# Moving the four block sums of each quad from VectorE to GpSimd in the last third of a fused attention + two-MoE kernel

## The chip, the cores and the metric

The kernel runs on one core of one Trainium2 chip. The metric is the device time of one execution in microseconds (us), taken as the median of several runs. The trace is of one profiled execution; its engines are called PE (TensorE matmuls; PEld its weight loads), DVE (VectorE), ACT (ScalarE), POOL (GpSimd) and SP (SyncE, which issues the DMAs here).

## What is computed

An attention without a score matrix feeds a first MoE layer (softplus) and a second one (ELU). The change lies in the last product, `g @ w_out` of the second layer:

```
def _moe2_ref(x, w_in, w_out) -> np.ndarray:
    h = x @ w_in
    alpha = 1.0
    g = np.where(h > 0.0, h, alpha * (np.exp(np.minimum(h, 0.0)) - 1.0))
    return (g @ w_out).astype(np.float32)
```

There are 2304 tokens, `d_model` is 512 and `d_ff` is 2048; everything is float32.

## The kernel before

Tokens are cut into six blocks of 384 (`BLK`), and the blocks into three pairs; `d_ff` is cut into eight slices of 256. One pair with one slice is a *quad*. Each layer goes pair by pair and, within a pair, slice by slice. A float32 product is done as three products of rounded halves (high by high, high by low, low by high), so each operand is split by a cast on ACT (the high half) and a subtraction on DVE (the low half).

The products with `w_in` (`add_up`, matmuls at L833) use a 2x2 block scheme with seven products in place of eight. In the second layer, the second and third pair (the trace calls them by p = 1 and 2; the change's words call them pairs 2 and 3) use such a scheme for `w_out` too. For these sixteen quads `add_elu` leaves g as two tiles of two blocks each, (B11, B21) and (B12, B22), 128x384 a block. `add_parts` then makes the seven left operands: three are blocks of g as they are, and four come from sums, done in place: S = B21 + B22 and B21 <- B11 - B21 ahead of product 7, B11 <- S - B11 ahead of product 6, and B12 <- B12 - B11 ahead of product 3 (L1116, one instruction each, both inputs in SBUF). Each operand is then split into a tile of a ring of six called F: the cast at L1135 (ACT), the subtraction at L1139 (DVE). `add_products` multiplies them by the ready right operands (matmuls at L1185, nine to an operand, in threes: two that read its high half, then one that reads its low half) in the order 1, 7, 6, 2, 5, 4, 3, for four quads at a time, so that the same six F tiles come round again and again: a tile is refilled when PE has used it, and used again five operands later. The four S tiles hold S until product 5.

The tiles live in memory that other rings have finished with, and the trace names them by those: the F tiles are `claim_q`, `claim_xq`, `claim_yl`, `claim_st`, `claim_k`, `claim_v`; the g tiles are `claim_u`, `claim_g`, `claim_gh`, `claim_gl`, `claim_ti`; S is `claim_raw` or `claim_y`. `claim_raw` is also the output tile, into which L1208 (ACT) and L1210 (DVE) bring the finished products from PSUM.

The other work of a quad that shares the engines: L846 and L852 (ACT) copy products of `w_in` out of PSUM, L867 (DVE) adds such a copy to a product in PSUM, L946 and L950 (ACT) and L960 (DVE) make the ELU, L603 (ACT), L607 and L614 (DVE) prepare the next pair's input.

Each step is recorded with an engine, an estimated duration (`t_dve`, `t_pool`), what it reads, writes and holds, and a due time. `Plan.order` then lists all steps: at each turn the step that can start first on its engine, late ones ahead. That list is the order of each engine's queue; on the chip each engine works in its order and waits on semaphores.

Of the kernel before, what the change touches and what calls it, by code (L numbers as in the profile page):

```python
# [15 lines left out]
PE, ACT, DVE, POOL, DMA = "PE", "ACT", "DVE", "POOL", "DMA"  # L16
# [130 lines left out]
def t_act(n, psum=False):  # L147
    return (0.051 if psum else 0.093) + n / 1200


def t_dve(n, fast=False):
    return 0.069 + n / (1920 if fast else 960)


def t_pool(n):
    return 0.15 + n / 476
# [7 lines left out]
def attention_moe_moe_kernel(  # L164
# [30 lines left out]
    nc = tc.nc  # L195
# [5 lines left out]
    BLK = P * R  # L201
# [40 lines left out]
    def step(eng, dur, r=(), w=(), make=(), due=None, after=0.0, behind=(), port=False, hold=(), line=None, tab=None):  # L242


        def add(fn):
            n = plan.add(eng, dur, fn, r, w, make, due, after, [*behind, last.get(line)], port, hold, tab)
            if line is not None:
                last[line] = n
            return n

        return add
# [818 lines left out]
    def slot(key):  # L1070
        T[key] = views[plan.tile_ring[key], plan.place[key]]
        return T[key]
# [17 lines left out]
    def halves(key):  # L1090


        slot(key)
        one = views.get(("F1", plan.place[key]))
        T[key] = (one, T[key]) if one is not None else (T[key][:, :BLK], T[key][:, BLK:])
        return T[key]
# [4 lines left out]
    def add_parts(m, p, i, f):  # L1101


        gk = [("g", m, p, f, j) for j in range(2)]
        sk, fk = ("S", m, p, f), ("F", m, p, f, i)
        A = [("A", m, p, f, n) for n in range(4)]
        b11, b21, b12, b22 = A
        block = lambda n: T[gk[n // 2]][:, n % 2 * BLK : (n % 2 + 1) * BLK]
        if i == 1:
            for n, key in enumerate(A):  # L1110
                plan.writer[key] = plan.writer[gk[n // 2]]

        def sum_(out, x, y, op, r, w, hold, make=()):
            @step(DVE, t_dve(BLK), r=r, w=w, make=make, hold=hold)
            def _():
                nc.vector.tensor_tensor(out(), x(), y(), op=op)  # L1116

        s = lambda: T[sk]
        if i == 7:
            sum_(lambda: slot(sk), lambda: block(1), lambda: block(3), ALU.add, [b21, b22], [], gk, [(sk, "S")])  # L1120
            sum_(lambda: block(1), lambda: block(0), lambda: block(1), ALU.subtract, [b11], [b21], gk[:1])
        if i == 6:
            sum_(lambda: block(0), s, lambda: block(0), ALU.subtract, [sk], [b11], gk[:1])
        if i == 3:
            sum_(lambda: block(2), lambda: block(2), lambda: block(0), ALU.subtract, [b11], [b12], gk)
        key, get, hold = {
            1: (b11, lambda: block(0), gk[:1]), 7: (b21, lambda: block(1), gk[:1]), 6: (b11, lambda: block(0), gk[:1]),
            2: (b12, lambda: block(2), gk[1:]), 5: (sk, s, []), 4: (b22, lambda: block(3), gk[1:]),
            3: (b12, lambda: block(2), gk[1:]),
        }[i]  # L1130
        fh, fl = ((x, m, p, f, i) for x in ("fh", "fl"))

        @step(ACT, t_act(BLK), r=[key], make=[(fk, "F")], w=[fh], hold=hold, line="F")
        def _():
            nc.scalar.copy(halves(fk)[0], get())  # L1135

        @step(DVE, t_dve(BLK), r=[key, fh], w=[fl], hold=[fk, *hold])
        def _():
            nc.vector.tensor_tensor(T[fk][1], get(), T[fk][0].bitcast(F32), op=ALU.subtract)  # L1139
# [326 lines left out]
```

## Time and profile before

| what | value |
|---|---|
| median of 3 runs | 832.95 us (832.44 to 833.37) |
| the profiled execution: its time | 833.62 us |
| its span, first to last instruction | 831.9 us |
| mean granted TensorE clock | 0.998 of full speed |
| busy: PE, PEld | 809.3 us (97%), 732.4 us (88%) |
| busy: DVE, ACT, POOL | 657.5 us (79%), 564.7 us (68%), 6.1 us (1%) |

Shares are of the span. What lies around the span is 833.62 - 831.9 = 1.7 us. Busy times of an engine count each instruction in full, although the next one starts a little before it ends (a 128x384 instruction of DVE lasts 0.55 us, and the next one starts 0.47 us after it).

### The profile page before, as it was taken

The numbers are of one execution on the slowest core, as the hardware profiler recorded it, in microseconds if no ns is written. First come the engines' busy times: TensorE is split into PE (matmuls) and PEld (weight loads), VectorE is DVE, ScalarE is ACT, GpSimd is POOL, SyncE is SP. The second block draws the span as 40 slices with busy tenths as digits, with TensorE's granted clock in tenths as the row PEclk, the third lists the DMA queues.
The fourth block names the chain that finished last, engine by engine and source line by source line (L and its number), as shares of the span: only waits on it lengthen the run. The fifth ranks groups of instructions, "written<-read, shape, count | busy, mean of one in ns | idle before, by whom it ended". The sixth has DMA issues, their size and how long they took to land.

```text
span 831.9 us, 13270 instructions
## 1 busy us (share of the span) xinstructions
PE 809.3 (97%) x5110; PEld 732.4 (88%) x5110; DVE 657.5 (79%) x1088; ACT 564.7 (68%) x889; POOL 6.1 (1%) x28
## 2 busy tenths in 40 slices
PE   5799999999999999999999999999999999999997
PEld 4455788888889999999999998898999999999997
DVE  7879999979887768777679788968468697766775
ACT  4878987876787856756657767667466675557552
POOL 2000000000000000000000000000000000000000
PEclk9999999999999999999999999999999999999999
DMA  9597786636985556576855898987687676787563
GB/s 288 155 284 234 225 283 197 196 115 206 284 263 215 181 206 236 206 253 221 321 191 218 289 371 331 328 325 242 239 311 292 234 284 222 271 278 301 202 225 147
DMA packets 75166, 205.33 MB, mean 247 GB/s; under 512 B 18784, under 2 KB 34144, under 8 KB 65632
## 3 DMA queue, kind: packets, MB, share of 16 engines
q1 hardware_dynamic: 75104, 204.49, 71.0%
q8 instruction: 40, 0.66, 0.3%
q14 instruction: 22, 0.18, 0.1%
HBM read 143.65 MB, written 60.82 MB: 246 GB/s over the span
## 4 chain that ended last, share of the span: by engine, by line
PE 82%; DVE 8%; ACT 5%; DMA 2%; issue 2%; DVEq 0%; ACTq 0%; SPq 0%
PE ub L833 21%; PE acc L1007 15%; PE acc L1045 13%; PE uc L833 11%; PE Pb L1185 8%; PE ua L833 5%; PE Pc L1185 4%; PE Pa L1185 2%; PE px L522 1%; DMA wf_i<-wfd 1%; DVE mt L346 1%; PE acc L1040 1%; PE pk L390 1%; DMA raw_i<-in_moe_w_in_dram 1%; PE pq L506 1%
## 5 line engine op out<-in xcount | busy, mean ns | idle before, releaser
L833 PE MATMUL ub<-xf,wf_i 128*128 128x384 f32 x1104 | 226.5, 339 | 1.4 <-ACT s L846 1.1
L833 PEld LDWEIGHTS ub<-xf,wf_i 128*128 128x128 f32 x1104 | 189.3, 188 | 13.4 <-ACT s L846 4.3
L846 ACT COPY s<-ub 128x384 f32<-128x384 f32 x138 | 65.8, 477 | 72.7 <-PE ub L833 71.6
L833 PE MATMUL uc<-xf,wf_i 128*128 128x384 f32 x552 | 111.8, 337 | 0.7 <-ACT g L916 0.7
L1007 PE MATMUL acc<-gh,wo_o 128*128 128x512 f32 (+1 forms) x512 | 111.7, 340 | 0.0
L1045 PE MATMUL acc<-wo_o,gh 128*128 128x512 f32 x336 | 106.7, 398 | 0.0
L833 PEld LDWEIGHTS uc<-xf,wf_i 128*128 128x128 f32 x552 | 95.1, 188 | 5.7 <-ACT g L916 1.9
L867 DVE TENSOR_TENSOR h<-uc,s 128x384 f32<-128x384 f32 x92 | 51.1, 555 | 52.6 <-PE uc L833 47.5
L1007 PEld LDWEIGHTS acc<-gh,wo_o 128*128 128x128 f32 x512 | 82.9, 188 | 7.3
L1045 PEld LDWEIGHTS acc<-wo_o,gh 128*128 128x128 f32 x336 | 61.4, 188 | 9.0 <-ACT yt L1295 0.2
L1045 PE MATMUL acc<-wo_o,gl 128*128 128x512 f32 x168 | 66.5, 396 | 0.0
L1007 PE MATMUL acc<-gl,wo_o 128*128 128x512 f32 (+1 forms) x256 | 65.5, 336 | 0.0
L973 DVE TENSOR_TENSOR gl<-g,gh 128x768 fp32r<-128x768 f32 x60 | 57.2, 953 | 8.4 <-ACT gh L969 8.3
L833 PE MATMUL ua<-xf,wf_i 128*128 128x384 f32 x276 | 56.0, 337 | 0.0
L969 ACT CAST gh<-g 128x768 fp32r<-128x768 f32 x60 | 50.2, 836 | 7.1 <-DVE g L960 6.3
L833 PEld LDWEIGHTS ua<-xf,wf_i 128*128 128x128 f32 x276 | 47.9, 188 | 1.4 <-ACT sx L535 0.3
L746 DVE TENSOR_TENSOR wf_i<-st_i,wf_i 128x1024 fp32r<-128x1024 f32 x30 | 36.7, 1222 | 15.1 <-ACT wf_i L742 15.1
L1007 PEld LDWEIGHTS acc<-gl,wo_o 128*128 128x128 f32 x256 | 39.1, 188 | 5.3
L916 ACT ACTIVATE g<-h 128x384 f32<-128x384 f32 (+1 forms) x44 | 30.2, 686 | 16.3 <-DVE h L867 16.1
L1045 PEld LDWEIGHTS acc<-wo_o,gl 128*128 128x128 f32 x168 | 31.5, 187 | 6.8
L742 ACT CAST wf_i<-r_i 128x512 fp32r<-128x512 f32 (+1 forms) x48 | 23.2, 511 | 16.5 <-PE uc L833 16.4
L742 ACT CAST wf_i<-st_i 128x1024 fp32r<-128x1024 f32 x30 | 31.4, 1048 | 1.1 <-DVE st_i L726 1.0
(282 smaller groups left out, 1429.2 us busy)
## 6 DMA issues: line engine op xcount, KB each, us to landing
wf_i<-wfd SPq DMA_DIRECT2D x16, 1792.0 KB, 8.2
ws<-wos SPq DMA_DIRECT2D x28, 1024.0 KB, 5.4
raw_i<-in_moe_w_in_dram SPq DMA_DIRECT2D x16, 1024.0 KB, 6.5
raw_o<-in_moe_w_out_dram SPq DMA_DIRECT2D x16, 1024.0 KB, 7.4
wo_o<-wod SPq DMA_DIRECT2D x14, 1024.0 KB, 5.5
wfd<-wf_i SPq DMA_DIRECT2D x8, 1792.0 KB, 7.8
r_i<-w32i SPq DMA_DIRECT2D x24, 512.0 KB, 6.0
wod<-wo_o SPq DMA_DIRECT2D x8, 1024.0 KB, 5.2
```

The costliest lines, as they stand in the source:

```text
L346: top = lambda o, x, y: nc.vector.tensor_tensor(o, x, y, op=ALU.max)
L742: nc.scalar.copy(view(0, lo, n, c), get())
L746: nc.vector.tensor_tensor(view(1, lo, n, c), get(), view(0, lo, n, c).bitcast(F32), op=ALU.subtract)
L833: nc.tensor.matmul(ps[:, :BLK], T[wk][:, lo : lo + P], T[xk][:, (2 * c + kc) * BLK : (2 * c + kc + 1) * BLK], start=(i in first and kc == ...
L846: nc.scalar.copy(new(sk), T[key][:, :BLK])
L867: nc.vector.tensor_tensor(T[hk][:, half * BLK : (half + 1) * BLK], T[key][:, :BLK], T[sk], op=ALU.add)
L916: nc.scalar.activation(o, i, AF.Softplus)
L969: nc.scalar.copy(new(hk), T[gk])
L973: nc.vector.tensor_tensor(new(lk), T[gk], T[hk].bitcast(F32), op=ALU.subtract)
L1007: nc.tensor.matmul(ps, T[wk][:, lo : lo + P], T[g][:, cols], start=(first and n == 0 and starts), stop=(f == NQ - 1 and j == 1 and n == 2) ...
L1045: nc.tensor.matmul(ps, T[g][:, col : col + P], T[wk][:, (2 * a + j) * DM : (2 * a + j + 1) * DM], start=(first and n == 0), stop=(f == NQ ...
L1185: nc.tensor.matmul(ps[:, x * 256 : x * 256 + 256], T[fk][a][:, r * P : (r + 1) * P], T[ck][:, q * 512 + b * 256 : q * 512 + b * 256 + 256] ...
```

## The change

```
@@ -1111,9 +1111,9 @@
                 plan.writer[key] = plan.writer[gk[n // 2]]
 
         def sum_(out, x, y, op, r, w, hold, make=()):
-            @step(DVE, t_dve(BLK), r=r, w=w, make=make, hold=hold)
+            @step(POOL, t_pool(BLK), r=r, w=w, make=make, hold=hold)
             def _():
-                nc.vector.tensor_tensor(out(), x(), y(), op=op)
+                nc.gpsimd.tensor_tensor(out(), x(), y(), op=op)
 
         s = lambda: T[sk]
         if i == 7:
```

The 64 sums go to POOL, with the planner's estimate for that engine, 0.15 + 384/476 = 0.96 us in place of 0.069 + 384/960 = 0.47 us. The planner makes its list anew. Apart from the numbers in names, the queues of PE and of SP come out as before; those of DVE and ACT change places here and there.

On DVE, where the first group of four quads of the second pair turns to its product 7 (rows of the difference; - is before, a space is both):

```order
 L1139 TENSOR_TENSOR claim_v_5818<-claim_u_5885,claim_v_5818 128x384
-L1116 TENSOR_TENSOR claim_y_6255<-claim_g_5925,claim_gl_5924 128x384
 L1139 TENSOR_TENSOR claim_q_3026<-claim_g_5906,claim_q_3026 128x384
-L1116 TENSOR_TENSOR claim_g_5925<-claim_g_5925 128x384
-L1116 TENSOR_TENSOR claim_g_5906<-claim_y_6244,claim_g_5906 128x384
-L1116 TENSOR_TENSOR claim_g_5925<-claim_y_6255,claim_g_5925 128x384
 L1139 TENSOR_TENSOR claim_xq_3365<-claim_g_5925,claim_xq_3355 128x384
```

Four sums leave DVE's queue between the low halves of product 7's operands. 

On DVE, where the last quad of all reaches `w_out` (the end of the program; `claim_gh_5959` and `claim_ti_5670` are its g):

```order
 L960 SCALAR_TENSOR_TENSOR claim_gh_5959<-claim_gh_5959,h_2_7_0_7996 128x768
+L960 SCALAR_TENSOR_TENSOR claim_ti_5670<-claim_ti_5670,h_2_7_1_8063 128x768
 L1139 TENSOR_TENSOR claim_st_5666<-claim_gh_5959,claim_st_5666 128x384
-L960 SCALAR_TENSOR_TENSOR claim_ti_5670<-claim_ti_5670,h_2_7_1_8063 128x768
 L1139 TENSOR_TENSOR claim_k_5810<-claim_gl_5960,claim_k_5810 128x384
 L1139 TENSOR_TENSOR claim_v_5818<-claim_u_5885,claim_v_5818 128x384
-L1116 TENSOR_TENSOR claim_y_6255<-claim_gh_5959,claim_ti_5670 128x384
 L1139 TENSOR_TENSOR claim_q_3026<-claim_ti_5729,claim_q_3026 128x384
-L1116 TENSOR_TENSOR claim_gh_5959<-claim_gh_5959 128x384
 L1210 TENSOR_TENSOR claim_raw_5748<-Pb_2_4_0_8107,claim_raw_5748 128x2x256
 L1210 TENSOR_TENSOR claim_raw_5748<-Pb_2_4_1_8115,claim_raw_5748 128x256
 L1139 TENSOR_TENSOR claim_xq_3365<-claim_gh_5959,claim_xq_3355 128x384
```

The second half of the last quad's ELU now stands ahead of the low half for `claim_st`, and the sums between the low halves are gone.

On ACT at the same place:

```order
 L1208 COPY claim_raw_5748<-Pb_2_0_0_7495 128x2x256
+L950 ACTIVATE claim_ti_5670<-claim_ti_5670 128x768
 L1135 CAST claim_st_5666<-claim_gh_5959 128x384
-L950 ACTIVATE claim_ti_5670<-claim_ti_5670 128x768
+L1208 COPY claim_raw_5748<-Pb_2_0_1_7505 128x256
 L1135 CAST claim_k_5810<-claim_gl_5960 128x384
-L1208 COPY claim_raw_5748<-Pb_2_0_1_7505 128x256
 L1135 CAST claim_v_5818<-claim_u_5885 128x384
 L1135 CAST claim_q_3026<-claim_ti_5729 128x384
```

The exponential of the last quad's second half goes ahead of the cast for `claim_st`.

## Rows read from the trace of the kernel before

**Rows 1.** The page: busy time of each engine, share of the span, instructions.

```profile
PE 809.3 (97%) x5110; PEld 732.4 (88%) x5110; DVE 657.5 (79%) x1088; ACT 564.7 (68%) x889; POOL 6.1 (1%) x28
```

**Rows 2.** Busy time of each engine from 594 to 830 us.

```profile
core 0: us, PE busy (x) PEld busy (x) DVE busy (x) ACT busy (x) POOL busy (x), PEclk, DMA share, GB/s
594.00:830.00 236.00, 232.15 (x1644) 230.41 (x1642) 170.22 (x305) 139.79 (x256) 0.00 (x0) 1.00 0.70 255
```

**Rows 3.** All waits of PE from 590 to 832 us: total, times, longest.

```profile
PE ub L833 <- ACT s L846: 0.8, 2, 0.6
PE ub L833 <- DMA wf_i<-wfd: 0.2, 1, 0.2
```

**Rows 4.** The chain that ended last, from 795 us: start, length, what.

```profile
795.95 5.36 PE Pb L1185 x45
...
822.83 3.95 PE Pb L1185 x33
...
826.80 0.69 DVE claim_raw L1210
```

**Rows 5.** DVE's busy time, 594 to 830 us: L1116, L1139, L960, L607, L614.

```profile
594.00:830.00 236.00, 34.74 (x64) 1.00 0.70 255
...
594.00:830.00 236.00, 60.27 (x111) 1.00 0.70 255
...
594.00:830.00 236.00, 29.57 (x31) 1.00 0.70 255
...
594.00:830.00 236.00, 6.68 (x7) 1.00 0.70 255
...
594.00:830.00 236.00, 3.80 (x4) 1.00 0.70 255
```

**Rows 6.** POOL's only two-input instructions (by line); then instructions around one of them.

```profile
L461 POOL TENSOR_TENSOR q<-q,qm 128x384 f32<-128x384 f32 x4 | 3.3, 828 | 17.9 <-DVE qm L454 17.0 <-DVE qd L476 0.9
...
16.83 0.83 POOL L461 TENSOR_TENSOR q<-q,qm 128x384 f32<-128x384 f32 x1 [0.92 <-DVE qd L476]
...
17.54 0.56 DVE L491 TENSOR_TENSOR q<-q,qd 128x384 f32<-128x384 f32 x1
...
17.69 0.52 ACT L467 ACTIVATE q<-q 128x384 f32<-128x384 f32 x1 [1.22 <-POOL q L461]
```

**Rows 7.** Instructions in order of time: mid stretch, DVE and then PE.

```profile
702.38 0.56 DVE L1139 TENSOR_TENSOR claim_yl<-claim_raw,claim_yl 128x384 fp32r<-128x384 f32 x1 [0.96 <-ACT claim_yl L1135]
...
713.36 1.23 PE L1185 MATMUL Pb<-ws,claim_yl 128*128 128x256 f32 x9
```

**Rows 8.** The same, first group of the second pair: DVE, then PE.

```profile
625.36 0.55 DVE L1139 TENSOR_TENSOR claim_st<-claim_g,claim_st 128x384 fp32r<-128x384 f32 x1
...
627.71 0.55 DVE L1116 TENSOR_TENSOR claim_g<-claim_g 128x384 f32<-128x384 f32 x1
...
634.11 1.24 PE L1185 MATMUL Pc<-ws,claim_xq 128*128 128x256 f32 x9
```

**Rows 9.** The same, last quad of all: DVE, ACT, PE.

```profile
798.34 0.56 DVE L1139 TENSOR_TENSOR claim_st<-claim_gh,claim_st 128x384 fp32r<-128x384 f32 x1 [0.93 <-ACT claim_st L1135]
799.09 0.96 DVE L960 SCALAR_TENSOR_TENSOR claim_ti<-claim_ti,h 128x768 f32<-128x768 f32 x1 [0.18 <-ACT claim_ti L950]
799.96 0.55 DVE L1139 TENSOR_TENSOR claim_k<-claim_gl,claim_k 128x384 fp32r<-128x384 f32 x1
...
803.24 0.55 DVE L1139 TENSOR_TENSOR claim_xq<-claim_gh,claim_xq 128x384 fp32r<-128x384 f32 x1
...
797.33 0.57 ACT L1208 COPY claim_raw<-Pb 128x512 f32<-128x512 f32 x1
797.79 0.51 ACT L1135 CAST claim_st<-claim_gh 128x384 fp32r<-128x384 f32 x1
798.21 0.84 ACT L950 ACTIVATE claim_ti<-claim_ti 128x768 f32<-128x768 f32 x1
...
800.07 1.24 PE L1185 MATMUL Pb<-ws,claim_st 128*128 128x256 f32 x9
801.15 1.24 PE L1185 MATMUL Pc<-ws,claim_k 128*128 128x256 f32 x9
802.23 1.24 PE L1185 MATMUL Pc<-ws,claim_v 128*128 128x256 f32 x9
...
804.36 1.24 PE L1185 MATMUL Pc<-ws,claim_xq 128*128 128x256 f32 x9
```

More of the change, by code (lines that the diff above doesn't have):

```diff
@@ L1113, in sum_ @@
         def sum_(out, x, y, op, r, w, hold, make=()):
-            @step(DVE, t_dve(BLK), r=r, w=w, make=make, hold=hold)
+            @step(POOL, t_pool(BLK), r=r, w=w, make=make, hold=hold)
             def _():
-                nc.vector.tensor_tensor(out(), x(), y(), op=op)
+                nc.gpsimd.tensor_tensor(out(), x(), y(), op=op)
         s = lambda: T[sk]
```

## The prediction

> **What bounds the kernel now.** I read the busy times first: PE is busy for 97% of the span and POOL for 1% [rows 1]. Then the stretch in which the sums lie, 594 to 830 us: PE is busy for 232.15 of 236 us at full clock, DVE for 170.22, ACT for 139.79, and POOL runs nothing at all [rows 2]. A busy PE alone proves little, so I read its waits: from 590 us on PE waits three times, 1.0 us in all, for a copy on ACT and for a transfer, and never for an F tile or a sum [rows 3]. The chain that ended last says the same: from 795.95 us it is PE's w_out products back to back up to the last one at 826.8 us, then one addition and the stores [rows 4]. So the end is set by PE's own work, which the change doesn't touch. Time can only be won out of that 1.0 us, and lost where a sum on POOL, or what stands behind it, makes PE wait.
>
> **What the change removes.** 64 sums leave DVE, 34.74 us of its busy time [rows 5], or 64 x 0.47 = 30 us of its queue. None of it lies on the chain, so it is worth nothing by itself; PE's own work hides it. Were DVE the bound, those 30 us would be the gain.
>
> **What it adds.** 64 instructions on POOL. The nearest row is POOL's own subtraction of two SBUF operands of 128x384, 0.828 us (one operand is repeated along its rows, which is the difference) [rows 6]; I take 0.83 us. That is 53 us in 236 on an engine with no other work there, so its queue is never full; no DMA is issued from it. Handing over is cheap: ACT started 0.03 us after that subtraction ended (16.83 + 0.83 = 17.66, then 17.69) [rows 6]. I count 0.08 us from a DVE or POOL result to POOL.
>
> **How much delay the F tiles bear.** In the steady stretch a low half is done long before its use: one started at 702.38 us and lasted 0.56, and PE reached the tile at 713.36, 10.4 us later [rows 7]. The six F tiles are refilled as PE frees them, and a sum in the middle of a group has its operands earlier still. A sum that takes 0.83 in place of 0.55 us, or even twice that, vanishes there. Two kinds of place remain: where the last quad of a group of four has just made its g and its sums are wanted at once.
>
> *The first group.* Both operands of the last quad's S were ready at about 625.4 us, but DVE, which works in order, came to the second sum only at 627.71; PE used the tile that hangs on it, `claim_xq`, at 634.11 [rows 8]. On POOL the sum has its own queue. Suppose the worst, that POOL starts only when DVE has done the four low halves in front, at 625.36 + 4 x 0.47 = 627.3 us plus 0.08: two sums (1.74), cast (0.54) and low half (0.57) end at 630.2, 3.9 us ahead of PE. The first tile of the stretch, `claim_st` at 625.36, hangs on no sum. Cost: nothing.
>
> *The last group.* Here nothing is interleaved any more and slack is smallest: the low half of `claim_xq` ended at 803.24 + 0.55 = 803.79, and PE came to it at 804.36 [rows 9]. PE's third matmul of the nine is the first to read the low half; nine take 1.08 us (801.15 to 802.23), so 0.24 us can be added to each slack. With the new order: ACT runs the exponential at 797.33 + 0.46 = 797.79, DVE the ELU at about 798.67, which ends at 799.62, 0.4 us earlier than before (0.96 us after 799.09). The low half of `claim_st` follows it, 799.54 to 800.09, where it ended at 798.90 before; PE needs it at 800.07 + 0.24 = 800.31. It fits by 0.2 us. Now the sums, in three cases:
> - No collision with DVE: S from 799.70 to 800.53, the second sum to 801.44, cast to 801.98, and the low half, behind two additions of L1210 that start once PE has closed `Pb` at 801.31, ends at 802.9. That is 0.9 us earlier than before.
> - POOL is kept out until DVE's four low halves end at 801.50: S and the second sum take 2 x 0.83 + 0.08, cast and low half 1.11, the end is at 804.35, and PE needs it at 804.36 + 0.24 = 804.60. Still no wait.
> - POOL gets in first and holds DVE for each whole sum: S from 800.09 to 800.92, the low half of `claim_k` ends at 801.47 where PE needs it at 801.39 (0.08 us late); a second sum then pushes `claim_v` to 802.85 against 802.55, 0.3 us late. The tiles behind have room. Cost: 0.4 us.
>
> The third and fourth sums are wanted later (product 6 and product 3 come 8 and 24 operands after product 1 in a group of four quads), and DVE has fewer instructions than before. From 0 to 0.4 us, nearer to nothing, because two of the three cases cost nothing; I take 0.1.
>
> **A rule that speaks against the change.** The only overlap of POOL with a two-input DVE instruction is 17.54 to 17.66 us, and DVE's took 0.56 us, no longer than usual [rows 6]; that is the tail of POOL's instruction and tells little. The Trainium skill, "SBUF — State Buffer", section "Who interferes with whom", states that a DVE instruction with two SBUF inputs and a GpSimd instruction that reads SBUF exclude each other for the whole instruction, whoever comes first. If it holds, the second and third case above are the true ones, and no trace shown here decides it. By rows alone it matters how much DVE work could collide: 60.27 + 29.57 + 6.68 + 3.80 = 100.3 us of two-input instructions stay on DVE [rows 5], 43% of the stretch. Even if every sum held DVE for its full 0.83 us, DVE would be taken for 170.22 - 34.74 + 53 = 188 of 236 us, or 80%: it would still keep up.
>
> **The sum.** 833.62 us for the profiled execution, minus 0 for DVE's relief, plus 0 in the steady stretch, plus 0 at the first group, plus 0.1 at the last: 833.7. The median of the runs shown lies 0.7 us below the profiled one, so 832.95 + 0.1, rounded: 833.1 us.
>
> **Rivals.**
> - *Slower: POOL's sums are much longer than its row.* The place is `claim_xq` of the last quad, the case in which POOL starts at 801.50. Two sums of T each end PE's slack when 801.50 + 2T + 1.19 passes 804.60, so at T = 0.955 us, and each us beyond costs 2 us. To pass 0.2% (1.7 us, about what a measurement of this kernel can tell from no change) T must be 1.8 us. A sum that always waited out one 768-wide ELU instruction would take 0.83 + 0.95 = 1.78: a loss of 1.65, 834.6 us. With T at three times its row, 2.5 us, the loss is 3.1, 836.1. For it: 43% of the stretch can collide. Against it: at that very place DVE has no two-input instruction to run, as it waits for the sum, and 0.83 us was steady over four instances (3.3 us in all).
> - *Faster: PE's 1.0 us of waits goes* [rows 3]. If DVE's relief brought ACT's copies forward, 832.0 us at best. Against it: two of the three waits are for L846, whose inputs come from PE, and the third for a transfer; none has a sum in front. It is also below the 0.2%.
> - *Held up in the queue of ACT.* A cast that waits for POOL stands ahead of L846 and L852, on which PE's next w_in products wait. If each of the four group ends lost 0.3 us so (a sum's excess of 0.28 over DVE's), 1.2 us: 834.2 us, still within 0.2%. For it: before, the casts behind the second sum ran right after it. Against it: POOL starts that sum earlier than DVE did.
>
> **How the numbers follow.** No change within 0.2%: 0.80 (the forecast with 0.68, the ACT queue with 0.08, part of the 1.0 us won with 0.04). Slower by more: 0.16 (T of 1.8 us or more with 0.12, several small waits on top of each other with 0.04). Faster by more: 0.04, for something that the trace doesn't show. The range reaches from 832.2 (the lowest run, 832.44, less a quarter of PE's waits) to 834.8 (the slower rival at T = 1.78 us, with 0.2 us of spread); I leave out 836 with the rest.
>
> **What would show it.** In the changed kernel's profile DVE is busy for some 35 us less, POOL for some 53 us more, and the end is the same: PE's waits from 590 us on stay near 1 us and none names L1116 or a claimed tile. The sums on POOL should last 0.83 us; if they last longer, or L1139 and L960 last longer or start late behind no semaphore, the two engines collide. In the last group the low half of `claim_xq` should end between 802.9 and 804.4 us. The prediction is wrong if PE shows waits at L1185 for ACT or DVE at 800 to 806 us, or if L846 starts late behind a cast that waits for POOL.

## The result, and the profile after

The changed kernel takes 838.42 us (median of 4 runs, 837.88 to 840.26) where the kernel before takes 833.16 (4 runs, 832.44 to 833.55): the ratio is 1.0068, with a 95% interval of 1.0050 to 1.0086. It is slower by 5 to 6 us, three times what 0.2% is, and lies above the range of 832.2 to 834.8. The profiled execution took 838.94 us with a span of 837.2, against 833.62 and 831.9 before, so the two traces show the same 5.3 us, at the same granted clock of 0.998.

The page, and the busy times of the stretch with the sums (the stretch is 5 us longer than in [rows 2] because the kernel is):

```profile
PE 811.3 (97%) x5110; PEld 732.1 (87%) x5110; DVE 647.9 (77%) x1024; ACT 564.3 (67%) x889; POOL 79.2 (9%) x92
...
594.00:835.00 241.00, 234.68 (x1646) 231.12 (x1644) 160.79 (x241) 139.88 (x257) 73.16 (x64) 1.00 0.69 249
```

64 sums have left DVE, which is 64 x 0.47 = 30 us of its queue (the records of neighbours overlap by 0.08 us, so that their 34.74 us count a little twice), yet DVE is busy for only 9.4 us less than in [rows 2] (170.22 minus 160.79). POOL is busy for 73.16 us, not 53. Where the rest of DVE's relief went shows line by line. Busy time of L1139, L960, L607, L614, and of L867, which has one operand in PSUM:

```profile
594.00:835.00 241.00, 79.16 (x111) 1.00 0.69 249
...
594.00:835.00 241.00, 30.53 (x31) 1.00 0.69 249
...
594.00:835.00 241.00, 7.57 (x7) 1.00 0.69 249
...
594.00:835.00 241.00, 4.49 (x4) 1.00 0.69 249
...
594.00:835.00 241.00, 24.87 (x45) 1.00 0.69 249
```

Against [rows 5], the same 111 low halves cost 18.89 us more, and the three other lines 0.96, 0.89 and 0.69: together 21.4 of the 30 us come back as longer instructions on DVE, which leaves 8.6, about the 9.4 seen. L867, the one with a single operand in SBUF, is no longer than it was in the kernel before:

```profile
594.00:830.00 236.00, 25.00 (x45) 1.00 0.70 255
```

**Where PE falls behind.** PE has the same instructions in the same order in both kernels, so the start of each can be taken from the start of the same one before. Before 600 us, where nothing was changed, this lag lies between -1.1 and 2.0 us in the executions of this document, so only its growth counts. It is counted from the first matmul that starts after 612 us: there the execution of the kernel before loses 0.43 us to a transfer of `wf_i` (the wait for DMA in [rows 3]), which no other execution does there, and all but 0.07 us of that is left out so. From there on it grows at three places and nowhere else: by 1.97 us from 612 to 640 (first group of the second pair), by 2.50 from 676 to 700 (the second group, where the third pair's input is prepared on DVE between the low halves), and by 0.89 from 798 to 808 (the last group). In the steady stretches between them it grows by nothing. The sum, 5.33 us with rounding, is the whole loss of the profiled execution.

PE's waits from 590 to 840 us name the first two places, and L1185 waits for nobody in this view:

```profile
PE ub L833 <- ACT s L846: 1.9, 3, 1.1
PE uc L833 <- DVE h L867: 1.0, 1, 1.0
PE ua L833 <- DVE h L867: 0.6, 1, 0.6
```

Against [rows 3] these are 3.5 us instead of 1.0, all before products of `w_in`, which hang on no sum. What they wait for is a copy or an addition that empties a PSUM bank. The view shows less than the lag because a wait inside a series of matmuls is recorded as a longer series.

**First group.** POOL, DVE, ACT and PE in order of time:

```profile
622.52 1.61 POOL L1116 TENSOR_TENSOR claim_y<-claim_g,claim_gh 128x384 f32<-128x384 f32 x1 [11.24 <-DMA out_dram<-y]
624.21 1.02 POOL L1116 TENSOR_TENSOR claim_g<-claim_g 128x384 f32<-128x384 f32 x1
625.31 1.61 POOL L1116 TENSOR_TENSOR claim_g<-claim_y,claim_g 128x384 f32<-128x384 f32 x1
626.88 1.33 POOL L1116 TENSOR_TENSOR claim_y<-claim_g,claim_gl 128x384 f32<-128x384 f32 x1
628.28 1.20 POOL L1116 TENSOR_TENSOR claim_g<-claim_g 128x384 f32<-128x384 f32 x1
...
625.97 1.37 DVE L1139 TENSOR_TENSOR claim_st<-claim_g,claim_st 128x384 fp32r<-128x384 f32 x1
627.26 1.36 DVE L1139 TENSOR_TENSOR claim_k<-claim_ti,claim_k 128x384 fp32r<-128x384 f32 x1
...
631.12 0.55 DVE L1139 TENSOR_TENSOR claim_xq<-claim_g,claim_xq 128x384 fp32r<-128x384 f32 x1
...
635.66 0.54 DVE L867 TENSOR_TENSOR h<-uc,s 128x384 f32<-128x384 f32 x1
...
629.52 0.52 ACT L1135 CAST claim_xq<-claim_g 128x384 fp32r<-128x384 f32 x1 [1.96 <-POOL claim_g L1116]
...
636.24 0.85 ACT L946 ACTIVATE claim_gl<-h 128x768 f32<-128x768 f32 x1 [1.80 <-DVE h L867]
...
638.54 0.49 ACT L846 COPY s<-ub 128x384 f32<-128x384 f32 x1
...
626.88 1.61 PE L1185 MATMUL Pb<-ws,claim_st 128*128 128x256 f32 x9
...
634.65 1.24 PE L1185 MATMUL Pc<-ws,claim_xq 128*128 128x256 f32 x9
639.09 1.15 PE L833 MATMUL ub<-xf,wf_i 128*128 128x384 f32 x5 [1.11 <-ACT s L846]
```

The same L867 and the same series of PE in the kernel before:

```profile
633.66 0.55 DVE L867 TENSOR_TENSOR h<-uc,s 128x384 f32<-128x384 f32 x1
...
626.70 1.24 PE L1185 MATMUL Pb<-ws,claim_st 128*128 128x256 f32 x9
```

While POOL runs sums back to back, each low half on DVE lasts 1.37 us instead of 0.55, one starting every 1.3 us, and each sum 1.2 to 1.6 us instead of the 1.02 us that a sum lasts alone. The extra 0.82 us has no releaser: it lies inside DVE's instruction. The first of these low halves is that of `claim_st`, which PE wanted at once: its series of nine takes 1.61 us instead of 1.24, so 0.37 us of the 1.97 are lost at a tile that hangs on no sum. Then the casts: ACT stands 1.96 us for the last quad's second sum. The low half of that operand ended at 631.67, and PE reached the tile at 634.65, so the tile itself was 3 us early, as predicted. But two L867 stood behind that low half in DVE's queue. The second started at 635.66 (633.66 before), the activation L946 behind it waited 1.80 us, and behind that in ACT's queue stood the copy L846 for which PE then waited; the lag grows by 1.38 us there. The remaining 0.28 us come at 620 us, where an L867 starts 0.43 us after the product that it waits for (0.08 before). The lag grows as much there in e3 below, in which nothing collides; the cause is open. (0.37, 1.38 and 0.28 are 2.03; the 0.07 of the transfer goes off.)

**Last group.** DVE, POOL, PE:

```profile
803.09 0.96 DVE L960 SCALAR_TENSOR_TENSOR claim_ti<-claim_ti,h 128x768 f32<-128x768 f32 x1 [1.26 <-ACT claim_ti L950]
803.96 0.55 DVE L1139 TENSOR_TENSOR claim_st<-claim_gh,claim_st 128x384 fp32r<-128x384 f32 x1
804.43 1.37 DVE L1139 TENSOR_TENSOR claim_k<-claim_gl,claim_k 128x384 fp32r<-128x384 f32 x1
805.73 1.36 DVE L1139 TENSOR_TENSOR claim_v<-claim_u,claim_v 128x384 fp32r<-128x384 f32 x1
807.01 1.36 DVE L1139 TENSOR_TENSOR claim_q<-claim_ti,claim_q 128x384 fp32r<-128x384 f32 x1
...
804.13 1.26 POOL L1116 TENSOR_TENSOR claim_y<-claim_gh,claim_ti 128x384 f32<-128x384 f32 x1 [6.85 <-DVE claim_ti L960]
805.47 1.20 POOL L1116 TENSOR_TENSOR claim_gh<-claim_gh 128x384 f32<-128x384 f32 x1
806.75 1.21 POOL L1116 TENSOR_TENSOR claim_gh<-claim_y,claim_gh 128x384 f32<-128x384 f32 x1
...
805.57 1.40 PE L1185 MATMUL Pc<-ws,claim_k 128*128 128x256 f32 x9
806.80 1.44 PE L1185 MATMUL Pc<-ws,claim_v 128*128 128x256 f32 x9
808.08 1.44 PE L1185 MATMUL Pc<-ws,claim_q 128*128 128x256 f32 x9
809.35 1.57 PE L1185 MATMUL Pc<-ws,claim_xq 128*128 128x256 f32 x9
```

Three sums and three low halves take turns. The four series of nine matmuls last 1.40, 1.44, 1.44 and 1.57 us, where three of them have 1.24 in [rows 9] and that of `claim_q` had 1.22:

```profile
803.31 1.22 PE L1185 MATMUL Pc<-ws,claim_q 128*128 128x256 f32 x9
```

PE loses 0.16 + 0.20 + 0.22 + 0.33 = 0.91 us inside the series, which is the 0.89 by which the lag grows.

### The profile page after: what moved, and what is told of

Same layout as the page of the kernel before. It is cut to its first block, busy times and chain, and to the rows that moved or that the text cites. A ratio compares the mean times of both kernels' runs of the same rounds, so it can differ in the third digit from the quotient of the medians.

```text
span 837.2 us, 13340 instructions
## 1 busy us (share of the span) xinstructions
PE 811.3 (97%) x5110; PEld 732.1 (87%) x5110; DVE 647.9 (77%) x1024; ACT 564.3 (67%) x889; POOL 79.2 (9%) x92
## 4 chain that ended last, share of the span: by engine, by line
PE 81%; DVE 11%; ACT 4%; issue 2%; DMA 1%; DVEq 0%; SPq 0%; ACTq 0%
PE ub L833 20%; PE acc L1007 14%; PE acc L1045 13%; PE uc L833 10%; PE Pb L1185 7%; PE ua L833 5%; PE Pc L1185 3%; PE Pa L1185 2%; PE acc L1040 2%; PE px L522 1%; DVE mt L346 1%; DVE xf L607 1%; DVE ts L614 1%; DMA w32i<-ti_i 1%; PE pq L506 1%
## 5 line engine op out<-in xcount | busy, mean ns | idle before, releaser
L846 ACT COPY s<-ub 128x384 f32<-128x384 f32 x138 | 65.8, 477 | 69.5 <-PE ub L833 68.3
L867 DVE TENSOR_TENSOR h<-uc,s 128x384 f32<-128x384 f32 x92 | 51.0, 554 | 56.4 <-PE uc L833 44.8
L1116 POOL TENSOR_TENSOR claim_raw<-claim_ti,claim_ti 128x384 f32<-128x384 f32 x1 | 1.0, 1021 | 376.8 <-DVE claim_ti L960 376.8
```

What stands on the lines that cost most here:

```text
L846: nc.scalar.copy(new(sk), T[key][:, :BLK])
L867: nc.vector.tensor_tensor(T[hk][:, half * BLK : (half + 1) * BLK], T[key][:, :BLK], T[sk], op=ALU.add)
```

## The experiments

The theory after this result has two parts. *Collision*: a sum on POOL and a DVE instruction with two SBUF operands exclude each other, and the low halves that are held come late or hold up what stands behind them. *Lateness*: a sum on POOL ends later than one on DVE would, and the cast or low half that waits for it holds up the copies and additions behind it on ACT and DVE, which empty PE's PSUM banks. The rival is *order*: the planner made a new list, and the list alone costs the time. A plainer rival is that POOL's work as such slows the others. Each kernel was compared with the kernel before on the same chip (833.25 us for e1 to e4, 832.56 for e5 to e8, 833.12 for e9 to e12).

The table gives the median, the ratio with its interval, and by how much PE's lag grew at the three places in the profiled execution (us). An execution's lag can also change by some 0.5 us elsewhere. The ratio is an estimate from all executions, so it differs a little from the quotient of the medians.

| kernel | us | ratio [95%] | 612-640 | 676-700 | 798-808 |
|---|---|---|---|---|---|
| after | 838.42 | 1.0068 [1.0050, 1.0086] | 1.97 | 2.50 | 0.89 |
| e1_old_order | 834.64 | 1.0022 [1.0013, 1.0031] | 1.32 | 0.75 | 0.03 |
| e2_new_order_dve | 834.95 | 1.0018 [1.0008, 1.0027] | 0.26 | 0.58 | 0.00 |
| e3_write_only | 833.25 | 0.9999 [0.9990, 1.0008] | 0.38 | -0.01 | 0.00 |
| e4_last_quad_dve | 835.93 | 1.0033 [1.0020, 1.0046] | 1.15 | 1.63 | 0.00 |
| e5_planner_knows | 835.72 | 1.0033 [1.0021, 1.0046] | 0.32 | 1.20 | 0.69 |
| e6_fill_same_waits | 836.10 | 1.0039 [1.0024, 1.0054] | 2.06 | 0.97 | 0.00 |
| e7_product3_only | 833.37 | 1.0005 [0.9995, 1.0015] | -0.10 | 0.00 | 0.00 |
| e8_last_quad_pool | 836.06 | 1.0036 [1.0023, 1.0050] | 1.03 | 0.69 | 0.91 |
| e9_idle_sums | 842.24 | 1.0105 [1.0088, 1.0121] | 3.31 | 5.57 | 0.59 |
| e10_first_group | 834.54 | 1.0020 [1.0008, 1.0031] | 1.96 | 0.00 | 0.00 |
| e11_second_group | 835.88 | 1.0027 [1.0016, 1.0039] | -0.02 | 2.51 | 0.01 |
| e12_last_group | 834.43 | 1.0015 [1.0002, 1.0027] | 0.53 | 0.01 | 0.92 |

**The engine without the order, and the order without the engine.** e1 runs the sums on POOL, but plans them as DVE steps, so that every queue keeps the order of before; e2 is the reverse.

```
 e1:  @step(DVE, t_dve(BLK), ...)     nc.gpsimd.tensor_tensor(out(), x(), y(), op=op)
 e2:  @step(POOL, t_pool(BLK), ...)   nc.vector.tensor_tensor(out(), x(), y(), op=op)
```

> The sums run on POOL, but the planner still counts them as DVE steps of 0.47 us, so that the queues of PE, SP, DVE and ACT keep the order of the kernel before (less the sums). Theory 1, collision: a sum on POOL and a DVE instruction with two SBUF inputs hold each other up, 0.8 us a time, whatever the planner's order; the time stays within 1.5 us of the changed kernel, 837 to 840 us, and L1139 keeps some 19 us of lengthening. Theory 2, order: the loss comes from the places that DVE's and ACT's steps changed in the new list; the time goes back to 833 to 834 us.

> The reverse: the planner counts the sums as POOL steps of 0.96 us and lists everything as in the changed kernel, but DVE executes them. Theory 1, collision: POOL does nothing here, so L1139 lasts 0.55 us again and the time is 832.5 to 834 us. Theory 2, order: the time stays slow, 836 to 839 us. If both have a part, something between, 834 to 836 us.

Neither alone gives the loss, and e1 lies in neither of its two ranges. In e1 the low halves take 76.78 us, so nearly all the collisions are there, and 1.8 us are lost (0.0022 x 833.25), most of it in the first group. In e2 they take 60.47 us, as before, and about 1.5 us are lost by the ratio. That is more than the order costs: e2's executions had a granted clock of 0.9969 on average where those of the kernel before had 0.9981 (which took 834.76 us at 0.995 and 832.18 to 833.26 at 0.999), and its 0.26 us in the first group is a wait of PE for the transfer of `wf_i`. What is left is, in the main, the 0.58 of the second group. Together e1 and e2 make some 3 us of the 5.3 at most; the other 2 us or more need both. The last group shows it best: 0.03 us and 0.00 apart, 0.89 together. With the old order the ELU's second half comes behind the low half of `claim_st`, POOL starts the sums later (0.4 us, measured from PE's series for `claim_st`), and only two of DVE's low halves meet them.

**POOL's work without the reading.** In e3 each sum is replaced by three fills of its output, which read nothing and wait for no operand; the products that use the sums are then of ones.

```
-                nc.gpsimd.tensor_tensor(out(), x(), y(), op=op)
+                o = out()
+                for _n in range(3):
+                    nc.gpsimd.memset(o, 1.0)
```

> Planned and placed as in the changed kernel, but each sum is replaced by three fills of the same block on POOL, which read nothing (the sums are left out, the output is not the reference's). Three fills should take 1.1 to 1.4 us, as long as a sum. Theory 1, collision in the reads of SBUF: L1139 lasts 0.55 us again although POOL is as busy, and the time falls to 833 to 834.5 us. Theory 3, lateness: what costs is only that a sum on POOL takes twice as long as on DVE and that casts on ACT wait for it; the time stays at 836 to 839 us. A fill waits for less than a sum does, so a part of a fall could also be that.

No loss clear of noise, with the new order and with POOL busy for longer (75.44 us). The low halves took (window from 594 to 833 us; L1141 here is L1139):

```profile
594.00:833.00 239.00, 60.24 (x111) 1.00 0.68 252
```

That is what they took in [rows 5]. So POOL's writing disturbs nobody. But e3 also took the sums' wait for their operands away, so the casts behind them came sooner. e6 puts that wait back: the first two columns are summed, then the block is filled three times.

```
+                o, a, c = out(), x(), y()
+                nc.gpsimd.tensor_tensor(o[:, :2], a[:, :2], c[:, :2], op=op)
+                for _n in range(3):
+                    nc.gpsimd.memset(o, 1.0)
```

> As the run with fills in place of sums, but each triple of fills is preceded by the sum of the first two columns, so that it waits for all that a sum waits for (the rest of each sum is left out, the output is not the reference's). It takes POOL longer than a sum, some 1.5 us. Theory 1 or 4, collision: reads of two columns hold nobody up for long, L1139 stays within 5 us of 60 and the time is 833 to 834.5 us. Theory 3, lateness: casts on ACT now wait for POOL as in the changed kernel or longer, and the time is 836 to 839 us.

The low halves stay at 60.07 us in all, so nothing collides, and yet 3 us are lost. ACT and PE's waits in e6:

```profile
629.97 0.52 ACT L1138 CAST claim_xq<-claim_g 128x384 fp32r<-128x384 f32 x1 [3.05 <-POOL claim_g L1119]
...
PE ub L833 <- ACT s L846: 2.2, 3, 1.4
```

It is the chain of the first group again, without a collision: with the new order, lateness is enough there (e3, the new order without it, has 0.38 us there). Its sums are longer than the real ones (1.6 to 2 us with the three fills), so its 2.06 us should be more than lateness costs in the changed kernel, where 0.37 of the 1.97 us is the held low half of `claim_st`. In the last group e6 loses nothing although the low half of `claim_xq` waits 1.31 us for ACT: there the loss is the collision.

**Which of the sums.** e4 leaves each group's last quad on DVE, e8 moves only that quad, e7 only the sum of product 3 (`i` counts the products, `f` the quads of a pair; cut: the step and its instruction then go to `eng`).

```
 e4:  eng = DVE if f % 4 == 3 else POOL
 e7:  eng = POOL if i == 3 else DVE
 e8:  eng = POOL if f % 4 == 3 else DVE
```

> Only the sums of the last quad in each group of four (16 of 64) go back to DVE; 48 stay on POOL. Theory 1 with the place that the changed kernel's waits of PE name (the end of each group, where four sums meet a row of low halves): most of the loss goes, 833.5 to 835.5 us, although 48 sums still collide in the stretch between. If the loss comes evenly from all collisions, a quarter of it goes: 836.5 to 838 us.

> Only the sums ahead of product 3 (16 of 64) run on POOL, the other 48 on DVE. Before, those ended 14 to 15 us ahead of their casts, and they lie spread over the stretch. Theory 1 and 4: they collide too, but behind each a low half with 10 us of slack is held, so 832.5 to 834 us. If each collision costs the same wherever it is, a quarter of the loss stays: 834 to 835 us.

> The other part of the fourth run: only the sums of the last quad in each group of four (16 of 64) run on POOL, 48 on DVE. If the group ends carry the loss, 836 to 838 us; if it needs the sums of the quads in front as well to push DVE's queue back (the run with those 48 alone on POOL lost 2.7 us), 833 to 835.5 us.

e7 costs nothing clear of noise: product 3 is the last of a group, and its operand has about 10 us to spare [rows 7]. e4 and e8 lose 2.8 and 3.0 us by the ratios, 2.78 and 2.63 by the table: together the whole loss, and e4 lies between its two ranges. So the three quads that I had put down as free carry about half of it, in the first two groups, and only the last group's loss hangs on its last quad alone.

**A planner that knows.** In e5 the sums, the low halves and the ELU (L960) of the quads that use the scheme are marked as steps that can't run at the same time on POOL and DVE (a flag that the planner already has). L607 and L614 are not marked.

```
-            @step(POOL, t_pool(BLK), r=r, w=w, make=make, hold=hold)
+            @step(POOL, t_pool(BLK), r=r, w=w, make=make, hold=hold, port=True)
...
-            make=[] if uk == gk else [(gk, "g")], line="g",
+            make=[] if uk == gk else [(gk, "g")], line="g", port=uk == gk,
...
-        @step(DVE, t_dve(BLK), r=[key, fh], w=[fl], hold=[fk, *hold])
+        @step(DVE, t_dve(BLK), r=[key, fh], w=[fl], hold=[fk, *hold], port=True)
```

> The changed kernel, but the planner is told that the sums on POOL, the low halves of L1139 and the ELU of L960 exclude each other (its flag for steps that share a port; the engines that execute them stay). Theory 4, collision times order: the collisions cost little where the queue is listed with them in mind; they cost 4 to 5 us only in a list made for a DVE that nobody holds up, where steps that free PSUM for PE come behind held ones. Then this version lies near the one with the old order, 833.5 to 835.5 us. Theory 1, collision alone: any list that keeps 64 sums on POOL pays for it, 836.5 to 839 us.

About half of the loss goes: 1.65 us in the first group and 1.3 in the second, and the time lies between the two ranges. It is still slower than before, so this list does not save the change. It isn't the best that could be tried: of the 1.20 us left in the second group, 0.87 arise where L614, which the planner did not know to collide, lasts 1.67 us ahead of an L867 for which PE then waits 0.61 us.

**Collision alone.** e9 is the kernel before, with its order and its sums on DVE, and behind each sum an idle subtraction of 128x384 on POOL for which nobody waits (`idle` is a tile made for this and filled once).

```
                 nc.vector.tensor_tensor(out(), x(), y(), op=op)
+                nc.gpsimd.tensor_tensor(idle[:, BLK:], block(3)[:, :2], idle[:, :2], op=ALU.add)
+                nc.gpsimd.tensor_tensor(idle[:, :BLK], idle[:, :BLK], idle[:, :BLK], op=ALU.subtract)
```

> The kernel before, unchanged in its sums and in every queue but POOL's: behind each sum on DVE, POOL reads two columns of that quad's B22 and then subtracts a tile of 128x384 of its own from itself, 64 times; nothing waits for its results. So collisions are there without lateness. Theory 1, collision: DVE's two-input instructions (L1139, L960 and the sums themselves) grow by 0.8 us each time, some 20 us or more in all, and since DVE keeps its 34 us of sums too, the time is 835 to 839 us. Theory 3, lateness: what cost was that ACT and DVE waited for sums on POOL; the time is 832.5 to 834 us even though DVE's instructions grow.

8.7 us are lost, more than either theory gave, and no engine waits for POOL anywhere in the stretch. DVE's sums (L1117 here) and low halves in the window from 594 to 840 us, and PE's waits:

```profile
594.00:840.00 246.00, 48.66 (x64) 0.99 0.67 244
...
594.00:840.00 246.00, 67.50 (x111) 0.99 0.67 244
...
PE uc L834 <- DVE h L868: 3.7, 3, 1.8
PE ub L834 <- ACT s L847: 2.1, 4, 0.8
```

The sums grew by 13.92 us and the low halves by 7.23. These are 44 held instructions, by 0.63 us each at most (in the changed kernel 33 low halves were held, by up to 0.82 us), and here DVE has the sums to do as well, so the queue in front of L867 is longer. Collision too is sufficient by itself.

**The three places one by one.** e10, e11 and e12 move the sums of one group each.

```
 e10: eng = POOL if p == 1 and f < 4 else DVE
 e11: eng = POOL if p == 1 and f > 3 else DVE
 e12: eng = POOL if p == 2 and f > 3 else DVE
```

> Sums on POOL only for the first group of four quads of the second pair, elsewhere on DVE. In the changed kernel PE fell back by 1.8 us between 612 and 639 us; the run with two-column sums and fills fell back as far there without long collisions. So lateness on POOL, and what stands in ACT's and DVE's queues behind the waiting cast, cost 1 to 1.8 us here: 834 to 835.2 us. If the place matters only with the queue pushed back elsewhere, 832.5 to 833.5 us.

> Sums on POOL only for the second group of the second pair, whose sums meet the forms of the next pair (L603, L607, L614) on DVE and ACT. In the changed kernel PE fell back by 2.5 us between 680 and 694 us. Collision and order: 1.5 to 2.5 us remain, 834.5 to 836 us. If it takes a queue pushed back by the first group, under 1 us: 832.8 to 833.8 us.

> Sums on POOL only for the last group of all. Three low halves are held there by three sums; PE fell back by 0.7 us from 801 us on in the changed kernel, and by as much in the run with the last quads alone. Collision: 0.6 to 1 us, 833.4 to 834.2 us, with PE reaching its tiles from claim_k to claim_xq late by 0.2 us each. The case of the prediction in which POOL gets in first gave 0.4 us.

1.96, 2.51 and 0.92 us, each at its own place: the table's three numbers for the changed kernel, to 0.03 us. (The median of e12 lies 0.2 us above its range; its growth at the place lies in it. The 0.53 of e12 in the first group lies at 621 us with the sums on DVE; its view of waits has 0.4 us for the transfer of `wf_i` there.) The losses are independent of each other and add up to 5.4 us, and the third group, which none of them moves, is free. PE's waits in e11 are those of the pair's turn:

```profile
PE uc L833 <- DVE h L867: 1.0, 1, 1.0
PE ub L833 <- ACT s L846: 0.8, 2, 0.6
PE ua L833 <- DVE h L867: 0.6, 1, 0.6
```

The second line is that of [rows 3]; the two for L867 are new. What makes L867 late shows in the changed kernel's DVE, ACT and PE at that place:

```profile
681.14 1.66 DVE L614 TENSOR_TENSOR ts<-sx,ts 128x768 f32<-128x768 f32 x1
682.73 0.54 DVE L867 TENSOR_TENSOR h<-uc,s 128x384 f32<-128x384 f32 x1
...
688.79 1.36 DVE L1139 TENSOR_TENSOR claim_k<-claim_ti,claim_k 128x384 fp32r<-128x384 f32 x1
...
692.77 0.54 DVE L867 TENSOR_TENSOR h<-uc,s 128x384 f32<-128x384 f32 x1
...
689.77 0.51 ACT L1135 CAST claim_v<-claim_g 128x384 fp32r<-128x384 f32 x1 [1.95 <-POOL claim_g L1116]
...
683.33 1.33 PE L833 MATMUL ua<-xf,wf_i 128*128 128x384 f32 x6 [0.61 <-DVE h L867]
693.37 1.33 PE L833 MATMUL uc<-xf,wf_i 128*128 128x384 f32 x6 [1.01 <-DVE h L867]
```

In the kernel before, the first two stood the other way round:

```profile
677.63 0.56 DVE L867 TENSOR_TENSOR h<-uc,s 128x384 f32<-128x384 f32 x1
678.10 0.95 DVE L614 TENSOR_TENSOR ts<-sx,ts 128x768 f32<-128x768 f32 x1
```

The new list puts L614 ahead of L867, and a sum on POOL makes L614 last 1.66 us; the lag grows by 0.87 us at PE's first wait. Seven us later held low halves, and one whose cast waited 1.95 us for a sum, stand ahead of another L867; the lag grows by 1.27 us at the second wait.

## Why the prediction was wrong

*What bounds the kernel, and DVE's relief is worth nothing.* Right. PE's own work still sets the end, and no run was faster than before beyond noise. Of the relief itself 21.4 of 30 us were given back.

*What it adds, 0.83 us for a sum.* Too low. A sum with two full operands lasts 1.02 us alone; the row of [rows 6] has one operand that repeats. With collisions the 64 took 73.16 us, 1.14 on average. By itself this was harmless.

*A rule that speaks against the change.* The Trainium skill, "SBUF — State Buffer", section "Who interferes with whom", was right here, in each part that a run tried: two-operand instructions of DVE were held, low halves for up to 0.82 us (0.55 to 1.37), L867 with one operand in PSUM was not (25.00 and 24.87 us), and fills that only write held nobody (60.24 us in e3). I named the rule, checked that DVE's total stayed below 80%, and stopped there. The total was never the question; the queue at three places was.

*How much delay the F tiles bear, and "The first group ... Cost: nothing".* This is the step that failed. Its own claim held for the tiles behind sums: the low half of `claim_xq` was ready 3 us before PE, in spite of POOL's late start (its first sum there stood 11.24 us, until a store had read `claim_y`'s memory, which I hadn't seen either) and, less the 0.2 us of lag at 625 us, 1.3 us later than I gave as the worst. It failed for `claim_st`, which I passed over as it "hangs on no sum": a sum held its low half, for 0.37 us of PE's time. Above all I asked only whether the delayed tiles reach PE in time. I did not ask what else stands in the queues of the instructions that are held or wait, and that was L867, L846 and L852, which empty the PSUM banks of PE's next `w_in` products. The term of the sum, "plus 0 at the first group", measured 1.97 us, 1.38 of it through these queues. The second group, with L607 and L614 in the same queue, I did not treat as a place at all, since its tiles have slack; it stood in "plus 0 in the steady stretch" and measured 2.50 us. These two are 4.5 of the 5.3 us.

*The last group.* The instants came out nearly to the digit. Less the 4.45 us of lag by then, the ELU's second half started at 798.64 us (I had 798.67) and S at 799.68 (799.70), and it was the third case, POOL first. Its price was too low, 0.4 for 0.89 us: I let two sums hold two low halves with 0.83 us each, and said that the tiles behind had room; three sums held three, and `claim_q` and `claim_xq` were late as well. The low half of `claim_xq` ended at 805.32 less the lag, not at 802.9 to 804.4. And I took 0.1, although the rule, if it held, struck out the first case, one of the two that cost nothing.

*The rivals.* "Held up in the queue of ACT" was the mechanism of the first group, with 0.3 us for each group end: 1.2 in all. It was right in kind, but it has to be taken for DVE's queue too and is no excess of a sum but a wait of 2 us; and what I held against it was wrong, since POOL came to the last quad's second sum at 628.28 us and DVE had at 627.71. "POOL's sums are much longer than its row" named the right direction at the wrong place: the sums were 1.0 to 1.7 us long, and the loss was not at their own tiles. The faster rival didn't come: two of PE's three waits in [rows 3] are for L846, and became longer.

*Open.* In the first two groups collision, lateness and the new order overlap, and the runs bound their shares but don't split them: in the second, order alone costs 0.58 us, POOL with the old order 0.75, lateness with the new order 0.97, all of it 2.50. No kernel here combines the old order with late but non-colliding sums. The 0.28 us at 620 us has no cause that the traces show. And a list that knows of most collisions (e5) still loses 2.7 us; a list that knows of those of L607 and L614 too was not tried.

## What to carry to other kernels

When work moves to an idle engine, look behind the instructions that will wait for it or be held by it: list what stands next in those queues, and above all the copies and additions that empty PSUM banks for the engine that sets the end. That the moved results have slack says nothing of them. And before counting an engine's relief as relief, see which of its remaining instructions have two operands in SBUF: a sum moved from DVE to POOL can cost DVE more, in a held instruction (up to 0.82 us), than it saved (0.47 us of its queue). Here 21.4 us for 64 sums are 0.33 us on average.

## What the runs showed of the hardware

- A collision leaves no wait in the trace. DVE's instruction starts on time and is recorded up to 0.82 us longer (0.55 to 1.37 us for 128x384, 0.94 to 1.66 for 128x768), with no releaser. When both queues are full the two take turns, one low half and one sum every 1.3 us, which is less work than DVE does alone in that time (1.3 / 0.47 = 2.8 instructions).
- Reading makes the difference. 192 fills of 128x384 on POOL lengthened nothing (e3), nor did they with a reading sum of two columns ahead of each three (e6).
- An addition of two full blocks of 128x384 lasts 1.02 us on POOL when nothing meets it, 0.83 us when one operand repeats along its rows (also the shortest of e9's idle subtractions, which have one block as both operands), and 0.55 on DVE.
